# A warm-up spin, a new load order and per-tile normalisation at the start of a fused attention-plus-MLP kernel

## The chip, the cores and the metric

The kernel runs on one core of one Trainium2 chip. The metric is the device time in microseconds (us) of one execution. Executions of this program spread by about half a per cent from one to the next, so the text gives a ratio with its 95% interval. A ratio is the mean time of one kernel's fast runs over the mean of the other's fast runs of the same rounds on the same chip, so it is not quite the ratio of the medians that stand beside it.

In the profile of the kernel before, TensorE (PE) does the matmuls (1113), VectorE (DVE, 259 instructions) and ScalarE (ACT, 95) elementwise work, GpSimd (POOL, 153) small elementwise work, and SyncE (SP) issues 75 of the 78 DMAs.

## The reference

```python
x  = A_x                                   # 2048 tokens x 448, bf16
xn = layernorm(x)
out = x + A(xn) + B(xn)
# A: feature-map attention (softmax features of q and k, 16 heads of 28), then @ wo
# B: h = gelu(layernorm(xn) @ w1); four column groups of h shifted by +-1, +-2 tokens; @ w2;
#    then x1 = xn + that; x1 + gelu(layernorm(x1) @ w3) @ w4
```

The tokens are handled as 16 tiles of 128. Only the start matters here: load x, normalise each tile, transpose it, and multiply it with wv (a "v block" of four tiles) and with w1 (a "w1 block" of four tiles).

## The kernel before

A recorder collects operations in program order for each engine and puts in the semaphore waits. In the traces VectorE then works through its own list in order (further down, it keeps tile 3 waiting 1.23 us behind a tile that has not landed), and this decides much of what follows.

```python
load_x(0, 1); load_x(1, 1); load_x(2, 2); load_x(4, 4)   # all on the SP queue
load_lap(w1, B_w1)                                       # SP
load_x(8, 4); load_x(12, 4)                              # SP
# ... w2, w_phi, eight DMA transposes of wqkv (SP) ...
load_lap(wv, A_wqkv[:, 896:1344], "ACT", mhalf)          # ScalarE's queue, behind a GpSimd memset
# ...
def ln1_stats(a, n, neg):
    for i in range(a, a + n):
        ln_stats(st, mv, xtok, i)        # VectorE: bn_stats, bn_aggr
    ln_scale(mv, rs, a, n, neg)          # GpSimd: 1/sqrt(var + eps) for n tiles
# ln1_apply(eng, i): xn = (x - mean) * rs, on VectorE (dve) or GpSimd (pool)

ln1_stats(0, 1, 0); ln1_stats(1, 1, 0); ln1_apply(dve, 0)
for i in (2, 3):
    ln1_stats(i, 1, 0)
    ln1_apply(dve, i - 1)
ln1_apply(dve, 3)
masks()                                  # GpSimd: five small operations
for i in range(4, NT, 2):                # tiles 4 to 15 in pairs
    ln1_stats(i, 2, 1)
    ln1_apply(pool, i)
    if i > 4:
        ln1_apply(dve, i - 1)
ln1_apply(dve, NT - 1)
xn_T(0, 0); xn_T(1, 1)                   # TensorE transposes, ScalarE copies out of PSUM
v_quad(0, ..., ([(xn_T, 2, 2)], [(xn_T, 3, 3)]))                  # transposes of later tiles
w1_quad(0, ..., ([], [], [(xn_T, 4, 4), (xn_T, 5, 5)], [...]))    # stand between the matmuls
v_quad(4, ...); w1_quad(1, ...)          # tiles 6 to 11 transposed in between; phi_blocks -> bd
for i in range(12, 16):
    xn_Td(i)                             # tiles 12 to 15 by DMA transpose (SP)
w1_quad(2, ..., folds of wpk); w1_quad(3, ..., folds of wpq)      # third and fourth w1 block
# ... the rest, 165 us ...
```

A "fold" is four small matmuls that build combined weights. I use two marks on TensorE's timeline: the **end of the first v block** (where the first w1 matmul starts), and **F**, the start of the first fold inside the fourth w1 block. From F to the end of the span, all 14 traces agree within 0.13 us (165.25 to 165.38), so F tells what the start of the kernel cost.

The softmax here doesn't subtract the row's maximum and nothing guards it: scores larger than these inputs give would overflow.

Of the kernel before, what the change touches and what calls it, by code (L numbers as in the profile page):

```python
# [5 lines left out]
ACT = mybir.ActivationFunctionType  # L6
ALU = mybir.AluOpType
# [10 lines left out]
class Recorder:  # L18
# [47 lines left out]
    def op(self, eng, fn, outs, ins, dma=False):  # L66
        w = set()
        r = set()
        for a in outs:
            w.update(self._keys(a))  # L70
        for a in ins:
            r.update(self._keys(a))
        self.ops.append((eng, fn, w, r, dma))

    def solve(self):
# [8 lines left out]
        for eng, fn, w, r, dma in self.ops:  # L84
# [40 lines left out]
            if not dma:  # L125
                s[eng] = pos[eng]
            snap[src] = s
            self.stream[eng].append((fn, todo, src, dma))
            waits.extend(todo)
            pos[eng] += 1  # L130
# [71 lines left out]
    def dma_t(self, out, in_, eng="SP"):  # L202
        self.op(eng, lambda e: e.dma_start_transpose(out, in_), [out], [in_], dma=True)  # L203

    def dma(self, out, in_, eng="SP", behind=None):
        self.op(eng, lambda e: e.dma_start(out, in_), [out], [in_] if behind is None else [in_, behind], dma=True)  # L206


def bass_parallel_sum__linear_kernel_hedgehog__mixer_s_mlp__prompt_kernel(
    nc, A_x, A_wqkv, A_w_phi, A_wo, B_x, B_w1, B_w2, B_w3, B_w4, out,  # L210
):
    _, S, D = A_x.shape
    H, DH = A_w_phi.shape[0], A_w_phi.shape[1]
    F = B_w3.shape[1]
    assert (S, D, H, DH, F) == (2048, 448, 16, 28, 1792)
    NT, NG, KC, NC, NM, FC, HP = 16, 4, 4, 4, 4, 14, 32
    CR = 112
    SHIFTS = [1, -1, 2, -2]
    HW = S + 8
    x2d, out2d = A_x[0], out[0]  # L220

    es = ExitStack()
    with es:
        R = Recorder(nc, es)
# [9 lines left out]
        def view(h, cols, dt=BF16, at=0):  # L234
            a = h[:, at // 2:at // 2 + cols * DTB[dt] // 2]
            return a if dt == BF16 else a.bitcast(dt)

        def new(name, cols, dt=BF16):
            return view(region(name, cols * DTB[dt]), cols, dt)
# [6 lines left out]
        banks = [pairs[b // 2][:, 512 * (b % 2):512 * (b % 2) + 512] for b in range(8)]  # L246


        xtok = new("xtok", NT * D).rearrange("p (t d) -> p t d", t=NT)
# [9 lines left out]
        gT = new("gT", 2 * KC * 512).rearrange("p (b c s) -> p b c s", b=2, c=KC)  # L259
# [4 lines left out]
        wv = new("wv", KC * D).rearrange("p (c d) -> p c d", c=KC)  # L264
# [4 lines left out]
        w1 = view(w1_r, KC * D).rearrange("p (c d) -> p c d", c=KC)  # L269
# [8 lines left out]
        maskb = new("maskb", CR)  # L278
        rsel = new("rsel", CR)
# [9 lines left out]
        mhalf = new("mhalf", 8, F32)  # L289
# [30 lines left out]
        def tview(b, n=512, base=0):  # L320
            return b[:, :].bitcast(BF16)[:, base:base + n]

        dve, pool = "DVE", "POOL"


        def load_x(i, n):
            R.dma(xtok[:, i:i + n, :], x2d[128 * i:128 * (i + n), :].rearrange("(j p) d -> p j d", p=128))

        def load_rows(dst, src):
            R.dma(dst[:, 0:3, :], src[0:384, :].rearrange("(c p) d -> p c d", p=128))  # L330
            R.dma(dst[0:64, 3, :], src[384:448, :])

        def load_lap(dst, src, eng="SP", behind=None):
            R.dma(dst[:, 0:2, :], src[0:256, :].rearrange("(c p) d -> p c d", p=128), eng, behind)
            R.dma(dst[:, 2:4, :], src[192:448, :].rearrange("(c p) d -> p c d", p=128), eng)

        load_x(0, 1)
        load_x(1, 1)
        load_x(2, 2)
        load_x(4, 4)  # L340
        load_lap(w1, B_w1)
        load_x(8, 4)
        load_x(12, 4)
        R.dma(w2[0:CR, :, :], B_w2.rearrange("(m p) d -> p m d", p=CR))
# [6 lines left out]
        def load_rest():  # L351
            load_lap(w3, B_w3)
            load_lap(wo, A_wo)
            R.dma(w4[:, :, :], B_w4.rearrange("(c p) d -> p c d", p=128))

        mb = maskb[0:CR, :].rearrange("p (h e) -> p h e", h=4)
        rv = rsel[0:DH, :].rearrange("p (h e) -> p h e", h=4)
        vp = vaug.rearrange("p t (h e) -> p (t h) e", e=HP)
# [5 lines left out]
                                             compare_op=ALU.not_equal, fill=1.0, base=0, channel_multiplier=1),  # L364
             [ident], [ident])
        R.ew(pool, "memset", mhalf[:, :], -0.5)
        load_lap(wv, A_wqkv[:, 896:1344], "ACT", mhalf)
        R.ew(pool, "memset", hT[:, :, 0:2], 0.0)
        R.ew(pool, "memset", hT[:, :, S + 2:S + 4], 0.0)
        R.ew(pool, "memset", vp[:, 0:8 * H, DH:HP], 0.0)  # L370
        R.ew(pool, "memset", vp[:, 0:8 * H, DH:DH + 1], 1.0)
        def masks():
            R.ew(pool, "memset", rsel[0:DH, :], 0.0)
            R.op(pool, lambda e: e.affine_select(rv, rv, pattern=[[0, 4], [-1, DH]], compare_op=ALU.not_equal,
                                                 fill=1.0, base=0, channel_multiplier=1), [rsel[0:DH, :]], [rsel[0:DH, :]])
            R.ew(pool, "memset", maskb[0:CR, :], 1.0)
            R.op(pool, lambda e: e.affine_select(mb, mb, pattern=[[-DH, 4], [0, DH]], compare_op=ALU.is_ge,
                                                 fill=0.0, base=0, channel_multiplier=1), [maskb[0:CR, :]], [maskb[0:CR, :]])
            R.op(pool, lambda e: e.affine_select(mb, mb, pattern=[[DH, 4], [0, DH]], compare_op=ALU.is_ge,
                                                 fill=0.0, base=DH - 1, channel_multiplier=-1),  # L380
                 [maskb[0:CR, :]], [maskb[0:CR, :]])

        def late_3():
            R.ew(pool, "memset", vp[:, 8 * H:NT * H, DH:HP], 0.0)
# [9 lines left out]
        def lap(a):  # L394
            return bass.AP(a.tensor, a.offset, [list(a.ap[0]), [192, 2], [1, 256]])

        def halves(a):
            return a.rearrange("p (b e) -> p b e", b=2)

        def ln_stats(stt, mvt, src, i):  # L400
            R.ew(dve, "bn_stats", stt[:, i, 0:6], src[:, i, 0:D])
            R.ew(dve, "bn_aggr", mvt[:, i, 0:2], stt[:, i, 0:6])

        def ln_scale(mvt, rst, a, n, neg):
            R.ew(pool, "tensor_scalar", mvt[:, a:a + n, 2], mvt[:, a:a + n, 1], LN_EPS, 1.0, op0=ALU.add, op1=ALU.mult)
            R.ew(pool, "tensor_tensor", rst[:, a:a + n, 0], mvt[:, a:a + n, 2], mhalf[:, 0:n], op=ALU.pow)
            if neg:
                R.ew(pool, "tensor_scalar", rst[:, a:a + neg, 1], mvt[:, a:a + neg, 0], -1.0, 0.0, op0=ALU.mult,
                     op1=ALU.add)

        def ln_apply(eng, dst, src, mvt, rst, i):
            m, op = (mvt[:, i, 0:1], ALU.subtract) if eng == dve else (rst[:, i, 1:2], ALU.add)
            R.ew(eng, "tensor_scalar", dst, src, m, rst[:, i, 0:1], op0=op, op1=ALU.mult)

        def ln1_stats(a, n, neg):
            for i in range(a, a + n):
                ln_stats(st, mv, xtok, i)
            ln_scale(mv, rs, a, n, neg)

        def ln1_apply(eng, i):  # L420
            ln_apply(eng, halves(xn[:, i, :]), lap(xtok[:, i, :]), mv, rs, i)


        def phi_blocks():
            b = banks[7]
            R.mm(b[0:CR, 0:D], rsel[0:DH, :], wphi[0:DH, :], True, True)
            R.ew(dve, "tensor_tensor", bd[0:CR, :].rearrange("p (c e) -> p c e", c=NC),
                 b[0:CR, 0:D].rearrange("p (c e) -> p c e", c=NC),
                 maskb[0:CR, :].unsqueeze(1).to_broadcast([CR, NC, CR]), op=ALU.mult)
# [8 lines left out]
        def xn_T(i, b):  # L438
            b = banks[b]
            for kc in range(KC):  # L440
                R.tr(tview(b)[:, 128 * kc:128 * kc + 128], xn[:, i, 128 * kc:128 * kc + 128], ident[:, :])
            R.act(xnT[:, :, 128 * i:128 * i + 128], tview(b).rearrange("p (c d) -> p c d", c=KC), ACT.Copy)
# [27 lines left out]
        def v_quad(i, bs, fills=()):  # L470
            quad(lambda k: banks[bs[k]][:, 0:D],
                 lambda k, kc, lo, hi: xnT[lo:hi, kc, 128 * (i + k):128 * (i + k) + 128],
                 lambda k, kc, lo, hi: wv[lo:hi, kc, :], fills)
            for k in (0, 2):
                vd = vaug[:, i + k:i + k + 2, :].rearrange("p t (h e) -> p t h e", e=HP)[:, :, :, 0:DH]
                vs = two(bs[k])[:, :, 0:D].rearrange("p t (h e) -> p t h e", e=DH)
                if i < 8:
                    R.act(vd, vs, ACT.Copy)
                else:
                    R.ew(dve, "tensor_copy", vd, vs)  # L480
# [135 lines left out]
            R.dma(out2d[128 * i:128 * i + 128, :], outb[:, i % 4, :])  # L616


        ln1_stats(0, 1, 0)
        ln1_stats(1, 1, 0)  # L620
        ln1_apply(dve, 0)
        for i in (2, 3):
            ln1_stats(i, 1, 0)
            ln1_apply(dve, i - 1)
        ln1_apply(dve, 3)
        masks()
        for i in range(4, NT, 2):
            ln1_stats(i, 2, 1)
            ln1_apply(pool, i)
            if i > 4:  # L630
                ln1_apply(dve, i - 1)
        ln1_apply(dve, NT - 1)
        xn_T(0, 0)
        xn_T(1, 1)
        v_quad(0, (4, 5, 6, 7), ([(xn_T, 2, 2)], [(xn_T, 3, 3)]))
        w1_quad(0, (0, 1, 2, 3), ([], [], [(xn_T, 4, 4), (xn_T, 5, 5)], [(xn_T, 6, 6), (xn_T, 7, 7)]))
# [84 lines left out]
        for h in range(2):  # L721
            c = slice(224 * h, 224 * h + 224)
# [32 lines left out]
```

## Time and profile before

| | before |
|---|---|
| time, median of the first 3 runs | 197.28 us |
| span of the profiled run | 195.5 us |
| TensorE busy | 94% |
| tiles 4 to 7 of x landed | 7.67 us |
| end of the first v block | 12.71 us |
| third w1 block: last matmuls end | 28.76 us |
| last DMA transpose (tile 15) landed | 29.24 us |
| F | 30.10 us |

Two lines of the page: busy time of each engine (us, share of the span, instructions), and the DMA queue whose kind the page gives as instruction.

```profile
PE 183.0 (94%) x1113; PEld 91.8 (47%) x1113; DVE 108.1 (55%) x259; ACT 81.1 (41%) x95; POOL 99.4 (51%) x153
...
q8 instruction: 9, 0.15, 0.3%
```

With TensorE busy 94% of the span, a start that lets TensorE begin sooner or reach its full clock sooner, or a removed wait, is what can shorten the kernel. (In before's trace the clock record turns to full at 10.89 us. 128x448 matmuls that follow one another start 373 ns apart until then and 190 ns apart from 10.97 us on; "cold" and "warm" below mean these two.)

The chain of waits that ended last (start in us, length in us, engine and what it did) shows the start of the kernel:

```profile
1.73 4.21 DMA xtok<-in_A_x_dram
5.96 0.64 DVE st L200
...
21.31 0.77 POOL xn L200
...
23.52 0.77 POOL xn L200
24.29 0.48 POOL vaug L200
24.76 1.19 SPq L203
26.00 3.24 DMA xnT<-xn
29.23 0.20 issue
29.43 8.81 PE bank L188 x56
```

From the load of tiles 2 and 3 the chain runs through VectorE and GpSimd, tile pair by tile pair, to the DMA transposes, and only at 29.43 us into TensorE. So before 29.4 us TensorE is not what ended last. How much sooner it was done is not in this view; the timeline of TensorE has it (start, length, operation, count, and in brackets the idle time before it and what ended it):

```profile
5.14 0.61 PE L192 MATMUL bank<-ident,xn 128*128 128x128 bf16 x4 [5.14 <-DVE xn L200]
7.56 1.33 PE L188 MATMUL bank<-wv,xnT 128*128 128x448 bf16 x3
12.71 2.15 PE L188 MATMUL bank<-xnT,w 128*112 128x512 bf16 x9
...
28.12 0.64 PE L188 MATMUL bank<-xnT,w 64*112 64x512 bf16 x4
29.43 0.83 PE L188 MATMUL bank<-xnT,w 128*112 128x512 bf16 x3 [0.67 <-DMA xnT<-xn]
```

TensorE waited 0.67 us. The SP queue's line for the four transposes is:

```profile
22.11 5.97 SPq L203 DMA_TRANSPOSE xnT<-xn  x4
```

### The profile page before, as it was taken

What the parts mean: (1) busy time and instruction counts of PE and PEld (TensorE: products, weight loads), DVE (VectorE), ACT (ScalarE), POOL (GpSimd) and SP (SyncE); (2) the same over time, 40 slices, a digit from 0 to 9 for tenths busy, and PEclk for the clock granted to TensorE, in tenths of its full rate; (3) what the DMA queues carried; (4) which work ended last, traced back from release to release, by engine and by line L of the source; (5) the groups of instructions that cost most, each with busy time, mean ns of one, the idle gap of its engine ahead of it and who ended that gap; (6) DMA issues with size and microseconds to landing.
All of it is one profiled execution on the core that took longest, in us unless ns stands there. A gap on an engine that the chain in (4) does not pass through costs nothing.

```text
span 195.5 us, 2884 instructions
## 1 busy us (share of the span) xinstructions
PE 183.0 (94%) x1113; PEld 91.8 (47%) x1113; DVE 108.1 (55%) x259; ACT 81.1 (41%) x95; POOL 99.4 (51%) x153
## 2 busy tenths in 40 slices
PE   0699989999999999999999999999999999999994
PEld 0346545445445454544445445454454445464451
DVE  3698500299959999975256527163173616756031
ACT  2359788944773666933451330033120330303000
POOL 5578850036792995894724334841435034276140
PEclk9999999999999999999999999999999999999999
DMA  5994249930020110005002431302243021222211
GB/s 131 373 226 87 50 84 334 354 115 0 2 54 3 27 27 0 3 0 107 0 0 54 84 68 23 91 4 74 53 84 77 24 50 27 54 50 61 63 50 47
DMA packets 32939, 14.74 MB, mean 75 GB/s; under 512 B 24670, under 2 KB 32414, under 8 KB 32926
## 3 DMA queue, kind: packets, MB, share of 16 engines
q1 hardware_dynamic: 32238, 14.04, 28.4%
q10 hardware_dynamic: 688, 0.52, 1.1%
q8 instruction: 9, 0.15, 0.3%
q14 instruction: 4, 0.03, 0.1%
HBM read 7.08 MB, written 1.84 MB: 46 GB/s over the span
## 4 chain that ended last, share of the span: by engine, by line
PE 77%; POOL 7%; DVE 5%; DMA 4%; ACT 3%; issue 2%; SPq 1%; DVEq 0%
PE bank L188 77%; POOL rs L200 3%; POOL xn L200 2%; DMA xtok<-in_A_x_dram 2%; ACT phik L196 2%; DVE vaug L200 2%; DMA xnT<-xn 2%; DVE st L200 1%; ACT eq_lo L196 1%; POOL phik L200 1%; POOL mv L200 1%; DVE xn L200 1%; SPq L203 1%; DVE ksum L200 1%; SPq L206 0%
## 5 line engine op out<-in xcount | busy, mean ns | idle before, releaser
L196 ACT ACTIVATE phik<-bank 128x1024 bf16<-128x1024 f32 (+1 forms) x44 | 40.9, 982 | 86.9 <-PE bank L188 86.9
L200 DVE TENSOR_TENSOR vaug<-bank,vaug 128x464 f32<-128x464 f32 (+3 forms) x65 | 32.7, 513 | 31.3 <-PE bank L188 29.7
L188 PE MATMUL bank<-gT,w 128*128 128x512 bf16 (+1 forms) x224 | 46.1, 380 | 0.7 <-ACT phik L196 0.7
L188 PE MATMUL bank<-w,phik 128*128 128x448 bf16 x224 | 45.1, 353 | 0.8 <-DVE vaug L200 0.8
L200 POOL TENSOR_TENSOR xnT<-vaug 128x196 bf16<-128x196 f32 (+1 forms) x32 | 18.1, 586 | 49.5 <-DVE vaug L200 49.5
L200 POOL TENSOR_TENSOR phik<-phik,rks 128x896 bf16<-128x896 bf16 x16 | 26.8, 1698 | 23.1 <-DVE rks L200 23.1
L188 PEld LDWEIGHTS bank<-w,phik 128*128 128x128 bf16 x224 | 21.0, 98 | 20.2 <-DVE vaug L200 1.7
L188 PEld LDWEIGHTS bank<-gT,w 128*128 128x128 bf16 (+1 forms) x224 | 17.7, 97 | 24.7 <-issue 5.9
L200 POOL TENSOR_TENSOR vaug<-xn,xtok 128x448 f32<-128x448 bf16 x16 | 16.4, 1030 | 5.1 <-DVE vaug L200 5.1
L200 DVE TENSOR_TENSOR xn<-bank,xn 128x256 bf16<-128x256 f32 (+1 forms) x32 | 10.7, 378 | 13.9 <-PE bank L188 13.6
L200 DVE TENSOR_REDUCE ksum<-phik 128x32 f32<-128x896 bf16 x16 | 16.8, 1051 | 0.0
L200 DVE RECIPROCAL vaug<-bank 128x16 f32<-128x16 f32 x16 | 4.1, 254 | 22.7 <-PE bank L188 22.7
L188 PE MATMUL bank<-xnT,w 128*112 128x512 bf16 (+1 forms) x64 | 15.1, 386 | 0.7 <-DMA xnT<-xn 0.7
L188 PE MATMUL bank<-xnT,wpq 128*112 128x512 bf16 (+1 forms) x64 | 14.9, 381 | 0.3 <-ACT eq_lo L196 0.3
L188 PE MATMUL bank<-wo,xnT 128*128 128x448 bf16 (+1 forms) x64 | 14.5, 352 | 0.0
L188 PE MATMUL bank<-w,hT 112*128 112x448 bf16 x64 | 14.3, 353 | 0.0
L188 PE MATMUL bank<-wv,xnT 128*128 128x448 bf16 (+1 forms) x64 | 14.1, 377 | 0.0
L188 PE MATMUL bank<-wpk,xnT 128*128 128x448 bf16 (+1 forms) x64 | 13.3, 355 | 0.0
L200 POOL TENSOR_SCALAR g_tok<-xn,rs 128x512 bf16<-128x512 bf16 x16 | 12.1, 772 | 0.0
L200 DVE BATCH_NORM_STATS2 st<-xtok 128x6 f32<-128x448 bf16 x16 | 9.7, 609 | 3.7 <-DMA xtok<-in_A_x_dram 3.7
L192 PE MATMUL bank<-ident,xn 128*128 128x128 bf16 x48 | 5.2, 250 | 6.6 <-DVE xn L200 6.6
L200 POOL TENSOR_TENSOR rs<-mv,mhalf 128x2 f32<-128x2 f32 (+2 forms) x14 | 10.5, 749 | 1.2
(58 smaller groups left out, 175.5 us busy)
## 6 DMA issues: line engine op xcount, KB each, us to landing
w<-in_B_w_dram SPq DMA_DIRECT2D x2, 896.0 KB, 5.8
out_dram<-vaug SPq DMA_DIRECT2D x15, 112.0 KB, 1.9
w<-in_B_w_dram SPq DMA_DIRECT2D x1, 1568.0 KB, 10.9
xtok<-in_A_x_dram SPq DMA_DIRECT2D x3, 448.0 KB, 6.1
wv<-in_A_wqkv_dram ACTq DMA_DIRECT2D x2, 224.0 KB, 4.3
w<-in_B_w_dram SPq DMA_DIRECT2D x2, 224.0 KB, 5.7
wo<-in_A_wo_dram SPq DMA_DIRECT2D x2, 224.0 KB, 6.9
w<-in_B_w_dram SPq DMA_DIRECT2D x1, 392.0 KB, 8.2
```

What stands on the lines that cost most here:

```text
L188: self.op("PE", lambda e: e.matmul(out, lhsT, rhs, start=start, stop=stop, skip_group_check=True), [out], [lhsT, rhs])
L192: self.op("PE", lambda e: e.transpose(out, in_, ident), [out], [in_, ident])
L196: self.op("ACT", lambda e: e.activation(out, in_, func, **kw), [out], [in_] + aps)
L200: self.op(eng, lambda e: getattr(e, name)(out, *args, **kw), [out], aps)
L203: self.op(eng, lambda e: e.dma_start_transpose(out, in_), [out], [in_], dma=True)
```

## The change

Its intent: let TensorE spin on a constant while the first tiles load, so that its clock is up when real work comes; issue x, wv and w1 on two queues in order of need; normalise tiles 0 to 7 one by one on VectorE, so that GpSimd has four pairs to do instead of six. For that, masks and memsets move ahead of the tiles. The diff, cut to its core:

```diff
         load_x(0, 1)
-        load_x(1, 1)
-        load_x(2, 2)
+        load_x(1, 1, "ACT")
+        load_x(2, 1)
+        load_lap(wv, A_wqkv[:, 896:1344], ("ACT", "SP"))
+        load_x(3, 1, "ACT")
         load_x(4, 4)
-        load_lap(w1, B_w1)
+        load_lap(w1, B_w1, ("ACT", "ACT"))
         load_x(8, 4)
 ...
-        load_lap(wv, A_wqkv[:, 896:1344], "ACT", mhalf)
-        R.ew(pool, "memset", vp[:, 0:8 * H, DH:HP], 0.0)        # and the 1.0 column
-        def masks(): ...
+        busy = gT[:, 0, 0, 0:256]
+        R.ew(dve, "memset", busy, 1.0)
+        R.ew(dve, "memset", vp[:, 0:8 * H, DH + 1:HP], 0.0)     # and the 1.0 column
+        ...                                                     # the masks, now at once
 ...
+        def spin(n, cols):
+            for _ in range(n):
+                R.mm(banks[3][:, 0:cols], busy[:, 0:128], busy[:, 0:cols], True, True)
 ...
-        ln1_stats(0, 1, 0) ... ln1_apply(dve, 3); masks()       # cut
-        for i in range(4, NT, 2):
+        for i in range(8):
+            ln1_stats(i, 1, 0)
+            if i > 0:
+                ln1_apply(dve, i - 1)
+        for i in range(8, NT, 2):
             ln1_stats(i, 2, 1)
             ln1_apply(pool, i)
-            if i > 4:
-                ln1_apply(dve, i - 1)
+            ln1_apply(dve, i - 1)
         ln1_apply(dve, NT - 1)
+        spin(17, 256)
         xn_T(0, 0)
+        spin(5, 128)
         xn_T(1, 1)
```

More of the change, by code (lines that the diff above doesn't have):

```diff
@@ L203, in dma_t, with dma @@
         self.op(eng, lambda e: e.dma_start_transpose(out, in_), [out], [in_], dma=True)
-    def dma(self, out, in_, eng="SP", behind=None):
-        self.op(eng, lambda e: e.dma_start(out, in_), [out], [in_] if behind is None else [in_, behind], dma=True)
+    def dma(self, out, in_, eng="SP"):
+        self.op(eng, lambda e: e.dma_start(out, in_), [out], [in_], dma=True)
 def bass_parallel_sum__linear_kernel_hedgehog__mixer_s_mlp__prompt_kernel(
@@ L323, in bass_parallel_sum__linear_kernel_hedgehog__mixer_s_mlp__prompt_kernel, with load_x @@
         dve, pool = "DVE", "POOL"
-        def load_x(i, n):
-            R.dma(xtok[:, i:i + n, :], x2d[128 * i:128 * (i + n), :].rearrange("(j p) d -> p j d", p=128))
+        def load_x(i, n, eng="SP"):
+            R.dma(xtok[:, i:i + n, :], x2d[128 * i:128 * (i + n), :].rearrange("(j p) d -> p j d", p=128), eng)
         def load_rows(dst, src):
@@ L331, in load_rows, with load_lap @@
             R.dma(dst[0:64, 3, :], src[384:448, :])
-        def load_lap(dst, src, eng="SP", behind=None):
-            R.dma(dst[:, 0:2, :], src[0:256, :].rearrange("(c p) d -> p c d", p=128), eng, behind)
-            R.dma(dst[:, 2:4, :], src[192:448, :].rearrange("(c p) d -> p c d", p=128), eng)
+        def load_lap(dst, src, engs=("SP", "SP")):
+            for h in range(2):
+                R.dma(dst[:, 2 * h:2 * h + 2, :], src[192 * h:192 * h + 256, :].rearrange("(c p) d -> p c d", p=128), engs[h])
         load_x(0, 1)
-        load_x(1, 1)
-        load_x(2, 2)
+        load_x(1, 1, "ACT")
+        load_x(2, 1)
+        load_lap(wv, A_wqkv[:, 896:1344], ("ACT", "SP"))
+        load_x(3, 1, "ACT")
         load_x(4, 4)
-        load_lap(w1, B_w1)
+        load_lap(w1, B_w1, ("ACT", "ACT"))
         load_x(8, 4)
@@ L366, in bass_parallel_sum__linear_kernel_hedgehog__mixer_s_mlp__prompt_kernel @@
         R.ew(pool, "memset", mhalf[:, :], -0.5)
-        load_lap(wv, A_wqkv[:, 896:1344], "ACT", mhalf)
         R.ew(pool, "memset", hT[:, :, 0:2], 0.0)
         R.ew(pool, "memset", hT[:, :, S + 2:S + 4], 0.0)
-        R.ew(pool, "memset", vp[:, 0:8 * H, DH:HP], 0.0)
-        R.ew(pool, "memset", vp[:, 0:8 * H, DH:DH + 1], 1.0)
-        def masks():
-            R.ew(pool, "memset", rsel[0:DH, :], 0.0)
-            R.op(pool, lambda e: e.affine_select(rv, rv, pattern=[[0, 4], [-1, DH]], compare_op=ALU.not_equal,
-                                                 fill=1.0, base=0, channel_multiplier=1), [rsel[0:DH, :]], [rsel[0:DH, :]])
-            R.ew(pool, "memset", maskb[0:CR, :], 1.0)
-            R.op(pool, lambda e: e.affine_select(mb, mb, pattern=[[-DH, 4], [0, DH]], compare_op=ALU.is_ge,
-                                                 fill=0.0, base=0, channel_multiplier=1), [maskb[0:CR, :]], [maskb[0:CR, :]])
-            R.op(pool, lambda e: e.affine_select(mb, mb, pattern=[[DH, 4], [0, DH]], compare_op=ALU.is_ge,
-                                                 fill=0.0, base=DH - 1, channel_multiplier=-1),
-                 [maskb[0:CR, :]], [maskb[0:CR, :]])
+        busy = gT[:, 0, 0, 0:256]
+        R.ew(dve, "memset", busy, 1.0)
+        R.ew(dve, "memset", vp[:, 0:8 * H, DH + 1:HP], 0.0)
+        R.ew(dve, "memset", vp[:, 0:8 * H, DH:DH + 1], 1.0)
+        R.ew(pool, "memset", rsel[0:DH, :], 0.0)
+        R.op(pool, lambda e: e.affine_select(rv, rv, pattern=[[0, 4], [-1, DH]], compare_op=ALU.not_equal,
+                                             fill=1.0, base=0, channel_multiplier=1), [rsel[0:DH, :]], [rsel[0:DH, :]])
+        R.ew(pool, "memset", maskb[0:CR, :], 1.0)
+        R.op(pool, lambda e: e.affine_select(mb, mb, pattern=[[-DH, 4], [0, DH]], compare_op=ALU.is_ge,
+                                             fill=0.0, base=0, channel_multiplier=1), [maskb[0:CR, :]], [maskb[0:CR, :]])
+        R.op(pool, lambda e: e.affine_select(mb, mb, pattern=[[DH, 4], [0, DH]], compare_op=ALU.is_ge,
+                                             fill=0.0, base=DH - 1, channel_multiplier=-1),
+             [maskb[0:CR, :]], [maskb[0:CR, :]])
         def late_3():
@@ L616, in store @@
             R.dma(out2d[128 * i:128 * i + 128, :], outb[:, i % 4, :])
-        ln1_stats(0, 1, 0)
-        ln1_stats(1, 1, 0)
-        ln1_apply(dve, 0)
-        for i in (2, 3):
+        for i in range(8):
             ln1_stats(i, 1, 0)
-            ln1_apply(dve, i - 1)
-        ln1_apply(dve, 3)
-        masks()
-        for i in range(4, NT, 2):
+            if i > 0:
+                ln1_apply(dve, i - 1)
+        for i in range(8, NT, 2):
             ln1_stats(i, 2, 1)
             ln1_apply(pool, i)
-            if i > 4:
-                ln1_apply(dve, i - 1)
+            ln1_apply(dve, i - 1)
         ln1_apply(dve, NT - 1)
+        spin(17, 256)
         xn_T(0, 0)
+        spin(5, 128)
         xn_T(1, 1)
```

## The prediction

> **What bounds the kernel now.** The page's busy shares put TensorE at 94%, and from about 29 us the chain of waits is nearly all TensorE. The change touches what comes before. There the chain of waits runs elsewhere: x lands (5.9 us), VectorE statistics, then from 10.9 to 24.3 us GpSimd's normalisation of tiles 4 to 15 in pairs (`mv` 0.20, `rs` 0.71, `rs` 0.20, `xn` 0.77 us: 2.2 us a pair, six pairs), then four DMA transposes of tiles 12 to 15, issued 1.3 us apart from 22.1 us (tile 12 ready), the last landing at 29.2 us. The fourth w1 block starts at 29.43 us. In the timeline TensorE had ended its third block at 28.76 us and idled 0.67 us; that block itself stood behind `bd` (24.4 us), behind the same pair chain.
>
> **What the change does, costed.**
> 1. Spin. [...]three 128x448 matmuls take 1.33 us at 7.6 us and 0.74 us at 42.8 us. The spin (estimate: 17x256 columns at half rate, 3.6 us, ending near 4.9 us, before tile 0's normalised rows at 5.1 us) delays nothing and shortens the first v block by some 2 us. But TensorE then waits for normalised tiles: off the critical path, worth about 0.
> 2. Tiles 4 to 7 one by one on VectorE: 1.10 us a tile in the timeline (0.62+0.18+0.40 us with overlaps). Tiles 0 to 7 take about 9 us from 2.9 us, and four GpSimd pairs remain instead of six. If no load is late, the first pair starts at about 13.2 us and tile 12 is ready at 19.8 instead of 22.1: 2.3 us gained.
> 3. Loads. Tile 2 no longer lands with tile 3 (5.94 us); VectorE's 0.9 us wait there goes. But w1 now shares the DMA engines with tiles 4 to 7 instead of queueing behind them. [...]about 375 GB/s in total from 4 us on, with one queue active or two. At half of that, tiles 4 to 7 land at about 7.9 us (7.67 before) while VectorE wants them at 7.1: 0.7 us is given back.
> 4. Memsets and masks moved between GpSimd and VectorE lie in slack: 0.
>
> **Sum.** Tile 12 ready at 20.5 us (-1.6), the last transpose lands at about 27.6, the fourth w1 block starts at 27.8; everything after moves by the same. 197.28 - 1.6 = 195.7 us; 8 in 10 between 194.6 and 196.7. Faster by over 2% (under 193.3) 0.03; within 2% 0.96; slower 0.01.
>
> **What would show it.** Early three-matmul groups take about 0.75 us; the first v block ends near 10.5 us (12.7). VectorE's statistics of tile 4 wait for x until about 7.9 us. GpSimd runs four pairs of 2.2 us from about 13.9 us. Transposes of tiles 12 to 15 still end the wait of the fourth w1 block, with TensorE idle about 1.2 us before it. After it the timeline is a shifted copy, about 166 us.
>
> **What would make it wrong.** Queues sharing unevenly (gain 0.8 to 2.4 us). ScalarE's five issues and table load (1.28 us) running past 6 us and holding the first copies. The transposes behind tile 12 were irregular (the fourth issue took 2.1 us): another run of them could move the result by up to 1 us. A later wait that depended on phase.

2.3 us (tiles 4 to 7) less 0.7 us (loads), with 0 for the spin and for the memsets, is the 1.6 us. The half rate of the spin's estimate is in before's trace: at 373 ns for 448 columns, cold, 17x256 columns come to 3.6 us. That a spin brings the full clock forward was the assumption.

## The result and the profile after

| | before | after |
|---|---|---|
| time, median (range) | 197.33 us (197.07 to 197.44), 4 runs | 196.27 us (195.78 to 196.62), 4 runs |
| ratio to before, 95% interval | | 0.9946 [0.9923, 0.9970] |
| span of the profiled run | 195.5 us | 194.5 us |
| tiles 4 to 7 of x landed | 7.67 us | 8.79 us |
| end of the first v block | 12.71 us | 12.26 us |
| last DMA transpose landed | 29.24 us | 27.99 us |
| F | 30.10 us | 29.29 us |

The gain is half a per cent, about 1.1 us, inside the predicted range. The page after:

```profile
PE 185.0 (95%) x1125; PEld 93.2 (48%) x1135; DVE 110.5 (57%) x264; ACT 81.0 (42%) x95; POOL 97.8 (50%) x151
```

The chain of waits after:

```profile
2.19 6.60 DMA xtok<-in_A_x_dram
8.82 0.64 DVE st L200
9.48 0.18 DVE mv L200
9.66 0.31 DVE xn L200
10.02 0.41 PE bank L192 x4
10.45 0.61 ACT xnT L196
11.10 3.31 PE bank L188 x16
...
27.78 0.54 ACT wpk L196
28.32 0.92 ACT hT L196
29.29 8.15 PE bank L188 x53
```

This is another chain. GpSimd and the DMA transposes are gone from it. It starts with the load of tiles 4 to 7, issued at 2.19 us and landed at 8.79, passes VectorE once, and from 10.02 us on it is TensorE with two short stops at ScalarE. The timelines of TensorE and of VectorE tell why the load of tile 4 holds the transpose of tile 3. First TensorE's:

```profile
1.26 3.81 PE L188 MATMUL bank<-gT 128*128 128x256 bf16 x17 [1.26 <-DVE gT L200]
6.75 0.73 PE L188 MATMUL bank<-wv,xnT 128*128 128x448 bf16 x3
10.02 0.40 PE L192 MATMUL bank<-ident,xn 128*128 128x128 bf16 x4 [1.41 <-DVE xn L200]
12.26 2.15 PE L188 MATMUL bank<-xnT,w 128*112 128x512 bf16 x9
29.29 0.37 PE L188 MATMUL bank<-bd,hi 112*128 112x112 bf16 x4 [0.20 <-ACT hT L196]
```

And VectorE's, of the same kernel, from the moment tiles 4 to 7 land:

```profile
8.82 0.63 DVE L200 BATCH_NORM_STATS2 st<-xtok 128x6 f32<-128x448 bf16 x1 [1.23 <-DMA xtok<-in_A_x_dram]
9.48 0.18 DVE L200 BATCH_NORM_AGGREGATE mv<-st 128x2 f32<-128x6 f32 x1
9.58 0.38 DVE L200 TENSOR_SCALAR xn<-xtok,mv,rs 128x512 bf16<-128x512 bf16 x1
```

The third VectorE line is tile 3's normalisation. In VectorE's list it stands behind tile 4's statistics, which wait 1.23 us for x. TensorE, warm by now (0.73 us for three matmuls, 1.33 before), therefore waits 1.41 us for tile 3. The warm array finished its early work sooner only to wait, and the first v block ends just 0.45 us earlier than before. The transposes on the SP queue are earlier, and shorter by 0.8 us, which needs an explanation of its own:

```profile
21.55 5.16 SPq L203 DMA_TRANSPOSE xnT<-xn  x4
```

At the end of the start a new wait has come in: the first fold of the fourth w1 block (F) waits 0.20 us for ScalarE's gelu of the third block, which frees its PSUM bank. Before, the wait for the transposes hid that.

### The profile page after: what moved, and what is told of

It reads as the page before. It is cut to its first block, busy times and chain, and to the rows that moved or that the text cites. A ratio compares the mean times of both kernels' runs of the same rounds, so it can differ in the third digit from the quotient of the medians.

```text
span 194.5 us, 2922 instructions
## 1 busy us (share of the span) xinstructions
PE 185.0 (95%) x1125; PEld 93.2 (48%) x1135; DVE 110.5 (57%) x264; ACT 81.0 (42%) x95; POOL 97.8 (50%) x151
## 4 chain that ended last, share of the span: by engine, by line
PE 85%; ACT 4%; DVE 3%; DMA 3%; issue 1%; POOL 1%; SPq 1%; DVEq 0%
PE bank L188 84%; DMA xtok<-in_A_x_dram 3%; ACT phik L196 2%; DVE vaug L200 2%; PE bank L192 1%; ACT eq_lo L196 1%; POOL phik L200 1%; SPq L206 1%; DVE ksum L200 1%; DVE xn L200 1%; ACT hT L196 0%; DVE st L200 0%; ACT xnT L196 0%; ACT wpk L196 0%; DVE rks L200 0%
## 5 line engine op out<-in xcount | busy, mean ns | idle before, releaser
L188 PE MATMUL bank<-gT,w 128*128 128x512 bf16 (+1 forms) x214 | 44.8, 380 | 1.2 <-ACT phik L196 0.7
L188 PE MATMUL bank<-wv,xnT 128*128 128x448 bf16 (+1 forms) x64 | 12.8, 353 | 0.1
L200 POOL TENSOR_TENSOR rs<-mv,mhalf 128x1 f32<-128x1 f32 (+2 forms) x16 | 11.3, 705 | 1.3
L200 DVE BATCH_NORM_STATS2 st<-xn 128x6 f32<-128x448 bf16 x16 | 9.4, 589 | 0.1
```

Of the source, the lines that this page charges most:

```text
L188: self.op("PE", lambda e: e.matmul(out, lhsT, rhs, start=start, stop=stop, skip_group_check=True), [out], [lhsT, rhs])
L200: self.op(eng, lambda e: getattr(e, name)(out, *args, **kw), [out], aps)
```

## The experiments

**Theory.** Two nearly level chains reach F. One is TensorE's own: cold or warm clock, and the wait for tile 3, set the end of the first v block. The other is normalisation, then the four DMA transposes. A part of the change that moves one chain alone gains little.
**Rivals.** The prediction's view: only the second chain counts, the spin is worth 0. A third reason came up from the traces: something other than normalisation makes the transposes slow in some of them.

All twelve kernels gave correct results. The table gives, for each profiled run: when tiles 4 to 7 landed, when TensorE's clock record turns to full, the end of the first v block, the time from the first issue of the four transposes to the last landing, F, and the median time and ratio to before of five rounds. The clock and landing times are read from the trace's records of clock and DMA. Each kernel has one trace. e1 to e4, e5 to e8 and e9 to e12 were timed as three sets on three chips, each beside its own 11 runs of before (medians 197.40, 197.31 and 197.17 us); the rows before and after repeat the result, 4 runs each. So kernels of one set can be set against each other directly, kernels of different sets only by their ratios.

| kernel | x 4-7 | full clock | v block end | transposes | F | median | ratio to before |
|---|---|---|---|---|---|---|---|
| before | 7.67 | 10.89 | 12.71 | 7.12 | 30.10 | 197.33 | |
| after | 8.79 | 5.03 | 12.26 | 6.44 | 29.29 | 196.27 | 0.9946 [0.9923, 0.9970] |
| e1: after, no spin | 9.18 | 10.78 | 12.81 | 7.06 | 29.84 | 196.79 | 0.9986 [0.9951, 1.0022] |
| e2: before + spin | 7.90 | 4.20 | 11.52 | 6.98 | 29.67 | 196.40 | 0.9955 [0.9934, 0.9977] |
| e3: after, w1 behind x | 7.80 | 4.13 | 11.26 | 6.49 | 28.30 | 195.90 | 0.9931 [0.9907, 0.9956] |
| e4: after, tile 3 first | 9.32 | 5.02 | 11.69 | 6.45 | 29.30 | 196.39 | 0.9955 [0.9934, 0.9976] |
| e5: e3 and e4 | 8.04 | 6.15 | 11.28 | 6.37 | 28.85 | 195.86 | 0.9924 [0.9909, 0.9939] |
| e6: before + tiny matmuls | 7.43 | 11.79 | 12.81 | 6.37 | 29.85 | 196.99 | 0.9978 [0.9961, 0.9995] |
| e7: after, spin made tiny | 8.06 | 9.62 | 11.89 | 7.20 | 28.93 | 196.58 | 0.9963 [0.9946, 0.9979] |
| e8: before + tile loop | 7.43 | 9.44 | 11.89 | 7.20 | 29.84 | 197.25 | 1.0001 [0.9977, 1.0024] |
| e9: tile loop + masks | 7.60 | 12.48 | 13.14 | 8.13 | 30.18 | 197.16 | 0.9981 [0.9951, 1.0011] |
| e10: after, old loads | 7.53 | 6.56 | 11.41 | 6.39 | 28.45 | 195.53 | 0.9926 [0.9896, 0.9956] |
| e11: before + new loads | 9.10 | no record | 12.14 | 7.40 | 30.12 | 197.11 | 0.9990 [0.9962, 1.0018] |
| e12: after, x ahead of wv | 8.78 | 5.09 | 13.95 | 6.40 | 30.98 | 198.36 | 1.0063 [1.0029, 1.0098] |

One regularity makes the table easy to read. In eight traces (after, e1, e3, e6, e7, e9, e10, e12), F comes 17.03 to 17.04 us after the end of the first v block. That is TensorE's own work with its fixed stops at ScalarE. Where F comes later than that (17.39 before, up to 18.15 in e2), TensorE also waited for a tile or for the transposes. So TensorE's chain alone would have put F at 12.71 + 17.04 = 29.75 us in before. It was at 30.10: **by this estimate perfect transposes alone could have gained 0.35 us.**

### e1_no_spin

```diff
-        spin(17, 256)
-        spin(5, 128)
```

> The kernel after without its 22 spin matmuls. Theory P (the prediction): the spin is off the critical path, worth about 0; the fourth w1 block still waits for its DMA transposes or for normalised tiles; time within 0.3 us of after (196.3). Rival Q (read from the trace after): TensorE runs without a real wait from tile 3's transpose at 10.0 us to the end, so a cold array costs there: ten 128x448 matmuls and some of the first w1 block at half rate add 0.7 to 1.7 us; time 197.0 to 197.9, no gain left over before. The first v block then ends after 13 us instead of 12.3.

Measured: 196.79 us (196.12 to 198.38), between the two expectations. F is 0.55 us later than in after, but 0.39 us of this is tile 3, whose wait for x was that much longer in this run (x landed at 9.18, not 8.79). That leaves 0.16 us for the cold array (the half rate of the expectation is the 373 ns against 190 ns of before's trace): it turned to full clock at 10.78 us, just when tile 3 came. So with the new load order most of what the spin warms up for is spent waiting for tile 3. The two time intervals overlap, so what removing the spin costs is not settled by time.

### e2_spin_only

```diff
+        busy = gT[:, 0, 0, 0:256]
+        R.ew(dve, "memset", busy, 1.0)
 ...
+        spin(17, 256)
         xn_T(0, 0)
+        spin(5, 128)
         xn_T(1, 1)
```

> The kernel before plus the spin and its VectorE memset, nothing else. Theory P: worth 0 here, because the GpSimd pair chain and the transposes of tiles 12 to 15 end the start (tile 12 ready at 22.1 us, fourth w1 block at 29.4 us): 197.1 to 197.4. Rival Q': TensorE was the limit before too: gain of 0.5 us or more.

Measured: 196.40 us, 0.45% faster than before, with the interval clear of 1. The expectation from the prediction (worth 0) fell. TensorE's lines, to be set against those of before:

```profile
9.51 2.08 PE L188 MATMUL bank<-wv,xnT 128*128 128x448 bf16 x10
11.52 2.15 PE L188 MATMUL bank<-xnT,w 128*112 128x512 bf16 x9
...
15.37 0.62 PE L192 MATMUL bank<-ident,xn 128*128 128x128 bf16 x8 [0.60 <-POOL xn L200]
...
29.01 0.83 PE L188 MATMUL bank<-xnT,w 128*112 128x512 bf16 x3 [0.65 <-issue]
```

The first v block ends 1.19 us earlier than before. Then TensorE waits 0.60 us for tile 6 from the GpSimd pairs, and later 0.65 us before the fourth block (the view names no releaser here; the last transpose had landed 0.09 us before): the warm array now runs into the other chain. Of 1.19 us, 0.43 us reach F. TensorE's own chain would have put F at 11.52 + 17.04 = 28.56 us, so in this trace the transposes set it: they landed at 28.92 us, 0.31 us sooner than in before. How the gain splits between the warm array and the earlier transposes is therefore not shown by this trace, which is also that of the slowest of e2's five runs (196.75 us).

### e3_w1_behind

```diff
-        load_lap(w1, B_w1, ("ACT", "ACT"))
+        load_lap(w1, B_w1)
```

> The kernel after with w1 issued on the SP queue behind x tiles 4 to 7 (as before) instead of on ACT. If the sharing of the DMA engines with w1 is what made tiles 4 to 7 land at 8.8 us: they land at 7.3 to 7.8 us, VectorE's 1.2 us wait there falls below 0.2 us, tile 3 is transposed about 1.1 us earlier, and the time falls by 0.7 to 1.1 us to 195.2 to 195.6. If the start is limited elsewhere (rival: TensorE's own work or the transposes): under 0.3 us.

Measured: tiles 4 to 7 land at 7.80 us instead of 8.79, tile 3 is transposed at 9.02 instead of 10.02, and F moves by 0.99 us, as expected of the theory:

```profile
9.02 0.40 PE L192 MATMUL bank<-ident,xn 128*128 128x128 bf16 x4 [0.28 <-DVE xn L200]
...
28.30 0.37 PE L188 MATMUL bank<-bd,hi 112*128 112x112 bf16 x4 [0.20 <-ACT hT L196]
```

The span is 193.7 us and the median 195.90 us, so 0.4 us by medians where 0.7 to 1.1 was expected; the ratios of e3 and after overlap. The landing varies from trace to trace: 8.06 to 9.32 us in the five with the change's load order, 7.80 and 8.04 in the two with w1 behind x, 7.43 to 7.90 in the six with the loads of before. So that the sharing with w1 held tiles 4 to 7 is well supported by the traces, though e7 (8.06) and e5 (8.04) all but meet.

### e4_apply3_first

```diff
         for i in range(8):
+            if i == 4:
+                ln1_apply(dve, 3)
             ln1_stats(i, 1, 0)
-            if i > 0:
+            if i > 0 and i != 4:
                 ln1_apply(dve, i - 1)
```

> The kernel after with tile 3's normalisation ahead of tile 4's statistics on VectorE. Tiles 4 to 7 still land at about 8.8 us. Tile 3 is transposed at about 8.9 us instead of 10.0, the first v block ends near 11.2 us (12.3). TensorE then waits for tile 7 (15.1 us in after, about 14.8 here, only 0.2 us before TensorE uses it there), so the gain is 0.2 to 0.4 us of the 1.1: 195.9 to 196.1. Rival: the wait for tile 3 alone is the limit, gain 1.0 us.

Measured: no gain over after (196.39 us, F at 29.30). Tile 3 was transposed at 9.45 us and the first v block ended at 11.69, but x landed at 9.32 us in this run, and TensorE then waited 0.40 us for tile 7, as the expectation feared. The rival (the wait for tile 3 alone is the limit) does not fit this trace: behind it stands tile 7, which hangs on the same load.

### e5_both

The edits of e3 and e4 together.

> The kernel after with both edits: w1 on the SP queue behind x tiles 4 to 7, and tile 3's normalisation ahead of tile 4's statistics. In e3 TensorE waited only 0.28 us for tile 3 and nothing after it until a 0.20 us wait for a gelu, so this adds at most 0.3 us to e3 (span 193.7, 195.9 us by rounds): 195.5 to 195.9. Rival: tile 7 comes later because tile 4's statistics move behind, no gain or a loss of 0.2 us against e3.

Measured: 195.86 us, with the narrowest spread of all (195.78 to 196.00). In its trace TensorE waited 0.36 us for tile 7, as the rival said, and F is at 28.85, later than e3's. By time it cannot be told from e3.

### e6_tiny_before and e7_tiny_after

Why were the four transposes 0.8 us shorter on the queue in after? Each DMA transpose takes about 1.27 us to issue. In before, one issue took 2.08 us and tile 14's transpose landed 4.0 us after its issue (28.73 us) where its neighbours took 2.5 to 3.2 us. The trace's DMA records show a 16,384-byte packet of the instruction queue (q8, nine packets on the page) at 26.70 us, in the midst of them. From one such packet to the next TensorE starts 174 to 284 recorded instructions in before (242 on average) and 229 to 269 in after (246). That these packets are TensorE's instruction fetch is my reading of this count; I call them the fetch from here on. Whether it delays the transposes is the question, since it falls among slow ones. The spin adds 44 instructions (22 matmuls and their weight loads), so by this reading the fetch should come earlier, and in after it does: at 19.36 us. The next two kernels keep the instruction count and take away the array work.

```diff
+        def tiny(n):
+            for _ in range(n):
+                R.mm(banks[3][0:16, 0:16], busy[:, 0:16], busy[:, 0:16], True, True)
 ...   # e6: in before, where the spin would stand; e7: in after, in place of the spin
+        tiny(17)
         xn_T(0, 0)
+        tiny(5)
         xn_T(1, 1)
```

> The kernel before plus 22 matmuls of 16x16 columns in the places of the spin (and the same VectorE memset): the same 44 instructions in TensorE's stream, next to no array work. Theory F (fetch): the spin in e2 helped because its instructions move TensorE's instruction fetch (a 16 KB packet, at 26.7 us in before, amid the transposes of tiles 12 to 15) to before them; then this gains as e2 did: 196.2 to 196.7, fetch packet before 22 us. Theory W (warm clock): e2 helped because the array was warm; then this stays at 197.2 to 197.5 and the full clock is reached near 11 us.

Measured for e6: 196.99 us, ratio 0.9978 [0.9961, 0.9995], between the two theories. The fetch came at 19.88 us and the transposes ran undisturbed:

```profile
21.84 5.15 SPq L203 DMA_TRANSPOSE xnT<-xn  x4
```

They landed at 28.21 us, 1.0 us sooner than in before, and TensorE no longer waited for them. But the array was cold until 11.79 us and the first v block ended at 12.81, so F is exactly TensorE's own 17.04 us later, at 29.85. **By time, 22 matmuls with next to no array work gain 0.22% [0.05, 0.39]**; that this is the fetch fits the trace. The rest of e2's 0.45% would be its warm array, whose first v block ended 1.29 us earlier than e6's, but this is not shown: the two were timed on different chips, their intervals overlap, and in e2's own trace the fetch came at 21.89 us, just as the first transpose was issued, and the four took 6.98 us. A cleaner measure of the warm array is e10 against e9, below.

> The kernel after with each spin matmul cut to 16x16 columns: same instruction count, no warm-up. Theory F: same as after, 196.2 to 196.5, with a narrow spread, and the fetch packet before 21 us. Theory W: same as e1 without any spin, 196.7 to 197.2, with the full clock near 10.8 us. In both the first v block's early groups of three matmuls take 1.33 us instead of 0.73.

Measured for e7: 196.58 us, between the two, and told apart from neither. It does beat before with a cold array, by 0.37% [0.21, 0.54]: most of after's gain may not need the warm array, as long as the new load order holds tile 3 back. Its profiled run (195.94 us, the fastest of six) had luck twice: x landed at 8.06 us and the clock was full at 9.62. Its fetch came at 22.12 us, among the transposes, against what theory F expected. What the spin's array work is worth inside after e7 does not settle.

Over all 14 traces the association is complete. (The limits were drawn after looking.) Where the fetch packet starts at or after the first issue of the transposes, give or take 0.1 us (before, e1, e2, e7, e8, e9, e11), the four take 6.98 to 8.13 us from first issue to last landing. In the other seven, where it is earlier, they take 6.37 to 6.49 us. Only e6 and e7 were made to test it, and e7's fetch came among the transposes all the same, so most of this is association. All five kernels without the 44 extra instructions had the fetch among the transposes, and only two of the nine with them (e2, e7). When exactly the fetch comes does not follow from the instruction count alone: before and e1 have the same TensorE program without a spin, and it came at 26.70 and 22.38 us. This stays open.

### e8_ln_only and e9_ln_masks

e8 puts the new loop over tiles 0 to 7 into before, with `masks()` after tile 3. e9 is after with the loads of before and without the spin, so with the loop and the moved masks and memsets.

```diff
         for i in range(8):
             ln1_stats(i, 1, 0)
             if i > 0:
                 ln1_apply(dve, i - 1)
+            if i == 3:
+                masks()              # e8 only; in e9 the masks come before tile 0
```

> The kernel before with the VectorE part of the change alone: tiles 0 to 7 one by one on VectorE (loads, memsets, no spin as before). Theory P: the GpSimd pair chain is the limit, tile 12 is ready 1.4 us earlier (20.7 us) and the transposes land by 27.3; TensorE's third block ends at 28.76 as before, so the fourth starts at 28.8 to 28.9 instead of 29.43: gain 0.5 us, 196.7 to 196.9. Rival: TensorE's third block also moves earlier because tiles 4 to 7 and the block-diagonal weights come earlier: gain 1.2 us or more, under 196.2.

Measured for e8: no gain (1.0001), tile 12 ready at 21.78 us and not 20.7. I had overlooked that the masks would now stand in the way: GpSimd did them from 8.5 to 10.1 us and VectorE waited 1.20 us for tile 4's scale factor. By chance its clock was full at 9.44 us without a spin, so TensorE's own chain would have put F at 11.89 + 17.04 = 28.93 us; the transposes, with the fetch among them at 25.92 us, landed at 28.98, and F came at 29.84. Here the second chain was the limit. The moved masks, which the prediction called free, are a condition for the loop. e9 removes that flaw.

> VectorE and GpSimd part of the change alone: per-tile normalisation of tiles 0 to 7 and the masks and memsets moved ahead, with the loads of before and no spin. Theory T (two chains nearly level): tiles 4 to 7 land at 7.4 to 7.9 us, tile 12 is ready near 20.8 us and the transposes are done by 27.3 (27.9 with an instruction fetch among them), but TensorE, cold until 9.4 to 11.8 us, ends its third block at 28.0 to 28.8 us, so the gain is 0.3 to 0.8 us: 196.5 to 197.0. Theory P (only the normalisation chain counts): fourth block at 27.5 us, 195.4 to 195.8.

Measured for e9: 197.16 us, 0.9981 with 1 inside the interval, a little less than even theory T expected. Tile 12 is ready at 20.69 us, 1.4 us earlier than before, as computed. And yet F is at 30.18:

```profile
10.40 2.81 PE L188 MATMUL bank<-wv,xnT 128*128 128x448 bf16 x10
13.14 2.15 PE L188 MATMUL bank<-xnT,w 128*112 128x512 bf16 x9
...
30.18 0.37 PE L188 MATMUL bank<-bd,hi 112*128 112x112 bf16 x4 [0.20 <-ACT hT L196]
```

TensorE was cold until 12.48 us, its first v block ended at 13.14 us, and 17.04 us later it reached F without waiting for any transpose. The transposes had landed at 28.82 us, with the fetch among them (26.67 us), 0.9 us later than the expectation allowed, and still before TensorE wanted them. This trace speaks against the prediction's view: tile 12 is ready over a microsecond sooner, and nothing comes of it, because TensorE's own chain, with the clock 1.6 us later than in before's trace, was the longer one. By time it is weaker evidence, since slow transposes alone would have left a gain of only some 0.4 us (28.82 against 29.24).

### e10_old_loads

after with the loads of before: x tiles 2 and 3 together, w1 behind x tiles 4 to 7 on SP, wv on ScalarE's queue behind the memset. Spin, loop and masks stay.

```diff
 ...   # the helpers' argument to wait behind a memset is put back (cut)
-        load_x(1, 1, "ACT")
-        load_x(2, 1)
-        load_lap(wv, A_wqkv[:, 896:1344], ("ACT", "SP"))
-        load_x(3, 1, "ACT")
+        load_x(1, 1)
+        load_x(2, 2)
         load_x(4, 4)
-        load_lap(w1, B_w1, ("ACT", "ACT"))
+        load_lap(w1, B_w1)
 ...
         R.ew(pool, "memset", mhalf[:, :], -0.5)
+        load_lap(wv, A_wqkv[:, 896:1344], ("ACT", "ACT"), mhalf)
```

> The kernel after with the loads of before (x on SP, tiles 2 and 3 together, w1 behind tiles 4 to 7, wv on ACT behind the GpSimd memset): the new load order alone is undone. If the new load order costs time (tiles 4 to 7 later by about 1.2 us): tiles 4 to 7 at 7.4 to 7.9 us, TensorE's wait for tile 3 gone, first v block ended by 11.6 us, 195.7 to 196.2, faster than after's 196.3. If the new order helps as intended: slower than after, 196.5 or more.

Measured: 195.53 us, a little under what was expected and the best median, ratio 0.9926. TensorE's lines:

```profile
9.17 0.40 PE L192 MATMUL bank<-ident,xn 128*128 128x128 bf16 x4 [0.17 <-DVE xn L200]
9.40 2.08 PE L188 MATMUL bank<-wv,xnT 128*128 128x448 bf16 x10
11.41 2.15 PE L188 MATMUL bank<-xnT,w 128*112 128x512 bf16 x9
...
28.45 0.37 PE L188 MATMUL bank<-bd,hi 112*128 112x112 bf16 x4 [0.20 <-ACT hT L196]
```

The wait for tile 3 falls from 1.41 to 0.17 us, and F comes 0.84 us earlier than in after. The new load order, as written, takes gain away. The intervals of e10 and after (0.9896 to 0.9956 and 0.9923 to 0.9970) overlap, so by time this is likely, and by the traces it is plain.

e10 is also e9 with the spin put in, and nothing else, timed in the same rounds on the same chip. The means of their six runs are 195.83 and 196.99 us: **with the loads of before, the spin is worth 1.15 us**, with a 95% interval of about 0.5 to 1.8 (Welch's t). Both traces reach F 17.04 us after the first v block without waiting for a transpose, and the block ends 1.73 us earlier (11.41 against 13.14), as does F. So the fetch plays no part in this difference of the traces: it is the clock, full at 6.56 us instead of 12.48.

### e11_loads_only

The load edits of the change alone, in before.

> The kernel before with the load order of the change alone. Tile 2 comes earlier (VectorE's 0.9 us wait at 5 us goes), tiles 4 to 7 later (8.8 to 9.3 us), but VectorE in before does not ask for tile 4 until 9.3 us. So the chain moves by 0 to 0.5 us: 196.9 to 197.4. If the order alone gives the gain: 196.3.

Measured: 197.11 us, not to be told from before, as expected. Tiles 4 to 7 landed at 9.10 us, the transposes (with the fetch among them) at 29.33, and F at 30.12.

### e12_x_first

```diff
         load_x(2, 1)
-        load_lap(wv, A_wqkv[:, 896:1344], ("ACT", "SP"))
         load_x(3, 1, "ACT")
+        load_lap(wv, A_wqkv[:, 896:1344], ("ACT", "ACT"))
         load_x(4, 4)
-        load_lap(w1, B_w1, ("ACT", "ACT"))
+        load_lap(w1, B_w1)
```

> A candidate to beat both: the kernel after with x tiles 0 to 3 ahead of wv on two queues, then wv on ACT and tiles 4 to 7 with w1 behind them on SP. Tile 3 by 5.2 us, tiles 4 to 7 by 7.2 us, wv by 6.9 us, VectorE never waits for x after tile 0, tile 3 transposed at 8.7 us (9.02 in e3), span 193.2 to 193.6, 195.2 to 195.7 by rounds. Rival: wv lands after 7 us and holds TensorE's first v matmuls, no better than e3 (195.9).

Measured: 198.36 us, slower than before. The rival was right and more. wv landed at 7.91 and 9.21 us, and TensorE sat waiting for it (0.87 and 0.86 us). It then lost the clock that the spin had gained, as the windows show (stretch, its length, busy time of the engines, granted clock, share and rate of the DMA engines):

```profile
5.00:8.50 3.50, 1.49 (x15) 0.83 (x14) 2.53 (x8) 1.19 (x2) 2.64 (x7) 1.00 1.00 308
8.50:12.00 3.50, 2.75 (x14) 1.62 (x15) 3.10 (x9) 0.60 (x1) 1.81 (x6) 0.51 1.11 321
```

The granted clock falls from 1.00 to 0.51, after a stretch in which TensorE was busy 1.49 of 3.50 us, with no pause over 0.9 us. (Where the trace has no clock record this column prints 1.00 as well, before 5.09 us here, so a cold start is read from the length of the matmuls and not from it.) My estimate of the landings was wrong by 1.6 us for tiles 4 to 7 (8.78 for 7.2) though they were issued sooner (1.72 us) than in any other kernel. The first of the 16 DMA engines had its share landed at 5.09 us and the last at 8.78.

## Why the prediction was right or wrong

The time was right: 196.27 us measured, 195.7 predicted, inside 194.6 to 196.7, and within 2% as forecast. The sum behind it was not. Two of its terms were wrong, and their errors partly cancelled, so that the number came out inside the range was in part luck.

1. **"Off the critical path, worth about 0"** (the spin) is the step that failed. The spin alone gains 0.45% [0.23, 0.66]. The fact it was built on held: the profile does show TensorE waiting 0.67 us for the transposes. But a chain that is 0.35 us from the limit (29.75 against 30.10) is not off the path once the other chain moves by more than that. In the prediction's own sum the warm array was needed for the 1.6 us, and it was booked at 0. With the loads of before the spin is worth 1.15 us (e10 against e9); with the new loads, which keep TensorE waiting for tile 3, the warm array may be worth much less (e7). A part of the spin's gain may come from a thing that I did not think of: its 44 instructions tend to move an instruction fetch out of the transposes' way (e6: at 19.88 us, for 26.70 in before).
2. **"2.3 us gained"** (tiles 4 to 7 on VectorE) was right as arithmetic for the normalisation chain: the pairs take 2.2 us each, and with the old loads tile 12 is ready at 20.7 us (e9, e10; 22.1 before). It was wrong as a gain. Without the spin it gives nothing that can be measured (e9). With the spin it shows in the traces: e10's F is 1.22 us ahead of e2's, though by time their intervals overlap.
3. **"0.7 us is given back"** (loads) had the right mechanism and too small a size. In these traces two queues together moved what one moved alone: from 7 to 8 us the SP queue moved 374 GB/s alone in before, and in after it moved 203 and ScalarE's queue 174, 377 together. In e3, taking w1 off the second queue brings tiles 4 to 7 from 8.79 to 7.80 us. Predicted landing 7.9 us; measured 8.79, 9.18, 9.32, 8.06 and 9.10 in the five traces with this load order. I had reckoned with half the rate and not with the 16 engines drifting apart: in after the first engine's share landed at 6.48 us and the last at 8.79, while before it was 7.03 and 7.67 (1.3 to 3.0 us apart in all five traces with this load order, 0.3 to 1.1 us in all six with the loads of before). VectorE waited 1.23 us instead of some 0.8, and GpSimd's pairs start at 14.92 instead of 13.9 us.
4. The consequence for TensorE was missed altogether. Tile 3's normalisation stands behind tile 4's statistics, so the late load also holds tile 3 and through it the first v block: 12.26 us, where the prediction said near 10.5.
5. **"Transposes of tiles 12 to 15 still end the wait of the fourth w1 block"** was wrong. They landed at 27.99 us, close to the predicted 27.6, and this too was luck: tile 12 was ready at 21.55 us, 0.56 us sooner than before and not 1.6, and the rest came from the four transposes running 0.68 us faster (6.44 us for 7.12), which the sum had not counted. TensorE's chain alone gives F at 12.26 + 17.04 = 29.30, measured 29.29, and the last short wait is for ScalarE's gelu.
6. Early groups of three matmuls at about 0.75 us (0.73) and the rest of the kernel as a shifted copy (165.37 us from F to the end before, 165.25 after) were right.

Without the spin the full clock came at 9.44 to 12.48 us in the six traces that record it, with the spin at 4.13 to 6.56 us; what sets the moment is not shown. Part of the half per cent of spread between executions may come from there; that is the author's estimate, not shown, since only one run of each kernel has a trace.

What stays open: how much the spin is worth inside after (e1 and e7 do not settle it), whether the fetch is what slows the transposes, and what sets its moment. Three variants, e3, e5 and e10, beat before by 0.7 to 0.8% with intervals clear of 1. Against after they are ahead in medians by 0.4 to 0.7 us, but were not timed in the same rounds, and their intervals overlap with its own.

## What to carry to other kernels

Before a term is booked at 0 because another chain ends later, measure how much later: if the change moves that other chain by more, the "free" part becomes the limit and the two have to be costed together. When a load moves to a second queue, look at what it will share the DMA rate with (here 377 GB/s over two queues, for 374 on one), and at what stands behind the delayed load in an engine's own list, because an in-order list passes the delay on to work that did not need that load (here VectorE's 1.23 us wait for tile 4 became 1.41 us of TensorE's for tile 3). Judge such small gains by marks in the trace (here the end of the first block and F) as well as by time, since the runs' own spread was as large as the gain; but take more than one trace where it matters, since with one load order x landed anywhere from 8.06 to 9.32 us.
